# Two small rows of the setup asked for behind ScalarE's table load instead of ahead of it

## The chip, the cores and the metric

The kernel runs on one core of a Trainium2 chip. The metric is the device time of one execution in microseconds (us), the median of several. Beside it stand the span (first to last instruction) of one profiled execution, and its trace.

## The reference, cut to what matters

One decoded token attends over a K and a V cache of 8 heads x 65536 rows x 256 numbers, and a small gated block runs beside it:

```python
xn = _layernorm(x, axis=-1)                       # x: 448 numbers
return x + _A_ref(xn, k_cache, v_cache, wq, wo)   # attention: q = xn @ wq, softmax(q k) v, @ wo
         + _B_ref(xn, w_r, w_gate, w_up, w_down)  # gated block, scaled by sigmoid(xn @ w_r)
```

The caches alone are 537 MB. The two rows are `x` (A_x) and `w_r` (B_w_r), 448 bf16 numbers or 896 bytes each. All the queries need `x`; the setup also reads `w_r` early.

## The kernel before

Each engine has its own list of instructions. `W` makes an engine wait for a named event, `O` adds an operation that signals its name, "d" is a transfer. SyncE asks for the big blocks, first wq, then K in halves:

```python
    item("wq", [(wq_area, flat_src(A_wq, WQN), "wq")])
    for u in range(U):
        k_item(u)          # blocks 0 and 1 at once; blocks 2 and 3 when TensorE has read the half before
    v_item(0)
```

A K block is 8.39 MB, a half 4.19 MB. Blocks 2 and 3 take the buffers of 0 and 1, so SyncE can ask for a half of them only when TensorE has transposed the half that lies there. ScalarE asks for the rows and then takes the square root of the layer norm:

```python
    def act_setup():
        a = nc.scalar
        for k, (d, s) in enumerate([(x_row, A_x[0]), (wr_row, B_w_r.rearrange("(o n) -> o n", o=1))]):
            prog["act"].append(("d", here[0], ("w0", k), (d, s), "w0"))
        items["w0"] = ("w0", 32)
        W("act", "VPE")
        O("act", "SQRT", lambda it: a.activation(out=stat[0:1, 3:4], in_=stat[0:1, 2:3], func=ACTF.Sqrt), "evq")
        ...
```

VectorE waits for both rows, converts `x` (`xf`), normalises; TensorE turns the row into columns (XNT), multiplies by wq (QT), and VectorE writes the queries (`qT_sb`). Meanwhile GpSimd writes constants and, last, fills `kt_all` with zeros:

```python
        O("pool", "z_q", lambda it: v.memset(q_cur[:, :, :], 0.0))
        O("pool", "KZ", lambda it: v.memset(kt_all[:, :], 0.0))
```

## Time and profile before

| | before |
|---|---|
| time, median of 3 (range) | 1277.45 us (1277.29 to 1277.73) |
| span of the profiled run | 1275.9 us |
| bytes moved, mean rate | 549.2 MB, 430 GB/s |
| DMA engines busy, by fortieth of the span | 9 tenths or more in 39, 8 in the last |
| rows seen by VectorE; queries ready; first K transposes | 7.06; 17.39; 22.68 us |

The page cuts the span into 40 slices with a digit of busy tenths for each engine, and lists the chain of work that ended last. The timeline gives start, duration, engine, source line and tiles, and in brackets the idle time before with what ended it. "SPq" and "ACTq" are requests for transfers.

### The profile page before, as it was taken

The numbers are of one execution on the slowest core, as the hardware profiler recorded it, in microseconds if no ns is written. First come the engines' busy times: TensorE is split into PE (matmuls) and PEld (weight loads), VectorE is DVE, ScalarE is ACT, GpSimd is POOL, SyncE is SP. The second block draws the span as 40 slices with busy tenths as digits, with TensorE's granted clock in tenths as the row PEclk, the third lists the DMA queues.
The fourth block names the chain that finished last, engine by engine and source line by source line (L and its number), as shares of the span: only waits on it lengthen the run. The fifth ranks groups of instructions, "written<-read, shape, count | busy, mean of one in ns | idle before, by whom it ended". The sixth has DMA issues, their size and how long they took to land.

```text
span 1275.9 us, 23521 instructions
## 1 busy us (share of the span) xinstructions
PE 956.1 (75%) x9744; PEld 627.2 (49%) x9744; DVE 570.5 (45%) x1078; ACT 436.6 (34%) x655; POOL 8.0 (1%) x38
## 2 busy tenths in 40 slices
PE   3998977678767769777778677687777698777664
PEld 3676655445544446444455454454444565444331
DVE  4665544445434455444454344454444544444310
ACT  1554533244322433324233243343333334332300
POOL 2000000000000000000000000000000000000000
PEclk9998998889888899888899888898888988887877
DMA  9999999999999999999999999999999999999998
GB/s 405 428 438 427 443 431 434 434 434 434 434 431 436 434 436 431 434 436 429 434 436 434 434 434 431 436 434 431 436 431 436 434 431 436 431 434 434 424 431 355
DMA packets 12886, 549.20 MB, mean 430 GB/s; under 512 B 1351, under 2 KB 1994, under 8 KB 3402
## 3 DMA queue, kind: packets, MB, share of 16 engines
q1 hardware_dynamic: 12868, 549.03, 99.7%
q8 instruction: 8, 0.13, 0.0%
q14 instruction: 4, 0.03, 0.0%
q10 hardware_dynamic: 6, 0.00, 0.0%
HBM read 549.03 MB, written 0.00 MB: 430 GB/s over the span
## 4 chain that ended last, share of the span: by engine, by line
DMA 78%; PE 18%; ACT 2%; issue 1%; DVE 1%; SPq 0%; ACTq 0%; DVEq 0%
DMA ring<-in_A_v_cache_dram 69%; PE ps_o L418 12%; DMA ring<-in_A_k_cache_dram 5%; PE ps_t L418 3%; DMA kt_all<-in_A_wo_dram 3%; DMA ring<-in_A_wo_dram 2%; PE ps_q L418 2%; ACT kt_all L479 2%; PE ps_m L418 1%; SPq L918 0%; DVE kt_all L477 0%; ACT S_sb L560 0%; DVE kt_all L720 0%; PE ps_s L418 0%; DVE kt_all L823 0%
## 5 line engine op out<-in xcount | busy, mean ns | idle before, releaser
L418 PE MATMUL ps_t<-ident_f,ring 128*128 128x128 f32 x4096 | 588.0, 285 | 83.3 <-DMA ring<-in_A_k_cache_dram 62.1
L477 DVE COPY kt_all<-ps_t 128x1024 bf16<-128x1024 bf16 x768 | 487.0, 685 | 294.0 <-PE ps_q L418 289.9
L418 PEld LDWEIGHTS ps_t<-ident_f,ring 128*128 128x128 f32 x4096 | 451.6, 144 | 235.8 <-issue 134.7
L479 ACT ACTIVATE kt_all<-ps_t 128x1024 bf16<-128x1024 bf16 x256 | 262.2, 1024 | 500.4 <-PE ps_q L418 500.3
L418 PE MATMUL ps_o<-ring,p_sb 128*4 128x512 bf16 x2044 | 173.6, 500 | 205.9 <-DMA ring<-in_A_v_cache_dram 201.6
L418 PEld LDWEIGHTS ps_o<-ring,p_sb 128*4 128x4 bf16 x2044 | 54.0, 101 | 290.3 <-issue 262.7
L418 PE MATMUL ps_q<-kt_all,q_cur 128*2 128x512 bf16 x2056 | 164.5, 397 | 0.3 <-DVE kt_all L477 0.3
L501 ACT ACTIVATE s<-ps_q 98x512 bf16<-98x512 f32 x257 | 151.8, 591 | 1.3 <-PE ps_q L418 1.3
L583 DVE RECIPROCAL rs<-ps_m 128x4 f32<-128x4 f32 x29 | 5.3, 183 | 273.3 <-PE ps_m L418 273.3
L570 ACT ACTIVATE p_sb<-S_sb 128x128 bf16<-128x128 bf16 x64 | 18.9, 307 | 262.4 <-PE ps_o L418 262.2
L418 PEld LDWEIGHTS ps_s<-sel_bf,s 128*128 128x128 bf16 x1032 | 64.0, 97 | 5.0 <-ACT s L501 1.9
L418 PE MATMUL ps_s<-sel_bf,s 128*128 128x8 bf16 x1032 | 63.3, 167 | 1.3 <-ACT s L501 1.3
L636 DVE CAST ob_sb<-ps_o 100x512 bf16<-100x512 f32 x29 | 20.1, 692 | 88.6 <-PE ps_o L418 88.6
L418 PEld LDWEIGHTS ps_q<-kt_all,q_cur 128*2 128x2 bf16 x2056 | 26.4, 79 | 45.1 <-issue 45.1
L418 PEld LDWEIGHTS ps_m<-rowsum,ones_f 128*128 128x128 f32 x58 | 12.0, 260 | 21.5 <-issue 21.5
L479 ACT ACT_TABLE_LOAD x7 | 9.0, 1283 | 27.6 <-PE ps_q L418 27.6
L530 DVE TENSOR_REDUCE m1p<-S_sb (+1 forms) x33 | 13.9, 422 | 4.4
L418 PE MATMUL ps_m<-rowsum,ones_f 128*128 128x4 f32 x58 | 14.6, 322 | 0.0
L528 DVE CAST S_sb<-ps_s 128x256 f32 (+1 forms) x33 | 13.7, 416 | 1.9 <-PE ps_s L418 1.9
L560 ACT ACTIVATE S_sb<-S_sb,negmax 128x512 bf16<-128x512 bf16 x16 | 13.2, 852 | 3.2 <-DVE negmax L554 3.2
L418 PE MATMUL ps_m<-diag,ones_f 2*128 2x2 f32 x58 | 11.2, 260 | 3.8 <-DVE diag L545 0.8
L418 PEld LDWEIGHTS ps_m<-diag,ones_f 2*128 2x128 f32 x58 | 8.7, 187 | 10.6 <-DVE diag L545 10.6
(95 smaller groups left out, 133.2 us busy)
## 6 DMA issues: line engine op xcount, KB each, us to landing
ring<-in_A_k_cache_dram SPq DMA_DIRECT2D x10, 4096.0 KB, 28.5
ring<-in_A_v_cache_dram SPq DMA_DIRECT2D x1, 4096.0 KB, 26.7
ring<-in_A_wq_dram SPq DMA_DIRECT2D x1, 3584.0 KB, 11.6
ring<-in_A_wo_dram SPq DMA_DIRECT2D x1, 2688.0 KB, 28.1
ring<-in_A_v_cache_dram SPq DMA_DIRECT2D x1, 2048.0 KB, 30.9
ring<-in_B_w_gate_dram SPq DMA_DIRECT2D x1, 1568.0 KB, 16.3
ring<-in_B_w_up_dram SPq DMA_DIRECT2D x1, 1568.0 KB, 19.5
ring<-in_B_w_down_dram SPq DMA_DIRECT2D x1, 1568.0 KB
```

The costliest lines, as they stand in the source:

```text
L418: return pe.matmul(*a, **k)
L477: O(e, ("EV", s, m), lambda it: nc.vector.tensor_copy(out=kt[:, :], in_=tb[:, :]), f"ev{m}")
L479: O(e, ("EV", s, m), lambda it: nc.scalar.activation(out=kt[:, :], in_=tb[:, :], func=ACTF.Copy), f"ev{m}")
L501: O("act", ("EVQ", s), lambda it: nc.scalar.activation(out=s2[s % 2][0:QROWS, :], in_=ps_q[0:QROWS, :], func=ACTF.Copy), "evq")
L528: O("dve", ("SCOPY", u), lambda it: nc.vector.tensor_copy(out=S_sb[:, at(it, SBN), :], in_=ps_sn), "sc")
L530: O("dve", ("SMAX", u), lambda it: nc.vector.tensor_reduce(out=m1p[:, :, at(it, 1)], in_=S_sb[:, at(it, SBN), :].rearrange("p n i -> p i n ...
L560: O("act", ("EXP", h, i), lambda it, i=i: nc.scalar.activation(out=S_sb[:, :, i], in_=S_sb[:, :, i], func=ACTF.Exp, bias=negmax[:, i:i + 1 ...
L570: O("act", ("PC", t, c), lambda it: nc.scalar.activation(out=p_sb[:, c, :, :], in_=S_sb[:, n:n + CH, :], func=ACTF.Copy), "pc")
L583: O("dve", ("RS", t), lambda it: nc.vector.reciprocal(out=rs[:, :, :], in_=ps_m[0:P, C_TOT:C_TOT + NH * rep]))
L636: O("dve", ("OB", t), lambda it: nc.vector.tensor_copy(out=ob_sb[0:OROWS, :], in_=ps_o[0:OROWS, :]))
```

## The change

The intent is that the function table of the square root is loaded at the very start of ScalarE's list, by a square root of one number that nobody reads, and that the rows are asked for after it. The root signals the same event as the rows, so those who wait for the rows count to 33 instead of 32. Whole:

```diff
     def act_setup():
         a = nc.scalar
+
+        W("act", "ones")
+        O("act", "TABLE", lambda it: a.activation(out=stat[0:1, 8:9], in_=ones_f[0:1, 0:1], func=ACTF.Sqrt), "w0")
+        W("act", "TABLE")
         for k, (d, s) in enumerate([(x_row, A_x[0]), (wr_row, B_w_r.rearrange("(o n) -> o n", o=1))]):
             prog["act"].append(("d", here[0], ("w0", k), (d, s), "w0"))
-        items["w0"] = ("w0", 32)
+        items["w0"] = ("w0", 33)
         W("act", "VPE")
```

## The prediction

> **What bounds the kernel now.** I read the page's slices first, since they say whether one resource is busy in every stretch.
>
> ```profile
> DMA  9999999999999999999999999999999999999998
> GB/s 405 428 438 427 443 431 434 434 434 434 434 431 436 434 436 431 434 436 429 434 436 434 434 434 431 436 434 431 436 431 436 434 431 436 431 434 434 424 431 355
> DMA packets 12886, 549.20 MB, mean 430 GB/s; under 512 B 1351, under 2 KB 1994, under 8 KB 3402
> ```
>
> In all but the first and last slices the sixteen DMA engines move 424 to 443 GB/s. 549.2 MB at 434 GB/s take 1265 us of the 1275.9 us span; ramp and tail hold the other ten. So the bound is the stream of transfers that SyncE issues (wq, then K and V blocks), and a change counts only if this stream starts later, runs dry or ends later. Next, the chain of waits, in order of time, for where compute enters it early on.
>
> ```profile
> 1.19 21.45 DMA ring<-in_A_k_cache_dram
> 22.68 1.97 PE ps_t L418 x8
> ...
> 81.08 1.04 PE ps_t L418 x8
> 82.14 37.95 DMA ring<-in_A_k_cache_dram
> 120.13 1.97 PE ps_t L418 x8
> ```
>
> TensorE starts its first K block at 22.68 us because that block's first half has landed; at 82.14 the chain goes back to a transfer. From 22.68 to 82.14 it names PE steps, which looks like a compute-bound stage. The table by stretches (columns: width, then busy us and count of PE, PEld, DVE, ACT, POOL, then the TensorE clock, DMA share and GB/s) corrects that:
>
> ```profile
> 0.00:22.68 22.68, 3.54 (x122) 3.41 (x123) 8.88 (x24) 2.97 (x4) 8.04 (x38) 1.00 0.95 391
> 22.68:82.14 59.46, 56.87 (x560) 41.91 (x560) 39.46 (x68) 29.95 (x43) 0.00 (x0) 1.00 1.00 431
> ```
>
> The transfers run at 431 GB/s there too: TensorE is merely busy beside them while blocks wait in the buffers. The third view is the timeline of the setup, which is what the change touches.
>
> ```profile
> 0.73 0.53 ACTq L918 DMA_DIRECT2D ring<-in_A_x_dram  x1
> 0.74 0.39 SPq L918 DMA_DIRECT2D ring<-in_A_wq_dram  x1
> ...
> 1.29 0.21 ACTq L918 DMA_DIRECT2D ring<-in_B_w_r_dram  x1
> ...
> 1.53 1.28 ACT L398 ACT_TABLE_LOAD   x1 [1.53 <-PEq L1131]
> ...
> 5.21 3.51 POOL L349 MEMSET kt_all<- 128x4096 bf16 x1
> 7.06 1.90 DVE L361 CAST ring<-ring 1x448 f32<-1x448 bf16 x1 [2.87 <-DMA ring<-in_B_w_r_dram]
> ...
> 17.20 0.19 DVE L409 TENSOR_SCALAR qT_sb<-ps_m 128x32 bf16<-128x32 f32 x1 [3.39 <-PE ps_m L418]
> 22.68 1.57 PEld L418 LDWEIGHTS ps_t<-ident_f,ring 128*128 128x128 f32 x8 [5.68 <-DMA ring<-in_A_k_cache_dram]
> ```
>
> The reader is to see the chain from rows to queries: rows asked for at 0.73 and 1.29, both there at 7.06, normalised on VectorE, multiplied by wq, queries ready at 17.20 + 0.19 = 17.39. Nothing can use them before the first K half at 22.68. The slack is 22.68 - 17.39 = 5.3 us, and the chain is not the one that sets the end.
>
> [...] the w_r row's 896-byte packet starts at 5.60 us, between packets of wq at 1.06 us each and long before wq is through at about 12.3; the 4-byte packet that signals it follows at 6.70, one wq packet later. So a small row passes a long queue, but not at once. [...] The five SyncE issues of the start are over by 1.19 + 2.11 = 3.30 us[...]. [...] The 1.28 us is in the trace[...]:
>
> ```profile
> 123.14 1.28 ACT L479 ACT_TABLE_LOAD   x1 [6.21 <-PE ps_q L418]
> 124.43 1.02 ACT L479 ACTIVATE kt_all<-ps_t 128x1024 bf16<-128x1024 bf16 x1
> ```
>
> The next function starts 1.29 us after the load does; I use 1.29. [...] The 1.90 us cast fits: it ends at 8.96, just after GpSimd's 5.21 + 3.51 = 8.72, and the opposite cast of the same 448 elements took 0.38 us.
>
> **The change part by part.** *Added:* one square root of one element, 0.20 us by its twin in the group rows, and a wait for the ones that GpSimd writes at 0.87 + 0.20 = 1.07 us. *Not added:* a table load, since that of the real square root moves to the new one. In the kernel before, the load ran at 1.53 though its function waited until 11.12, so it isn't held by the wait; I expect it at about 0.74, ending at 2.02, by when the ones are written. The function then ends at about 2.03 + 0.20 = 2.23. *Moved:* the row issues wait for it. The first goes from 0.73 to about 2.3, the second from 1.29 to about 2.8[...].
>
> Now the landing. Before, x was ahead of wq on an idle engine: packet at 1.64, 0.9 us after its issue. w_r (ready at about 1.29 + 0.9 = 2.2) arrived during the first wq packet of its engine (1.76 to 3.46) and got in at 5.60, after the third. After the change x is ready at 2.3 + 0.9 = 3.2, still inside that first packet, so at best it takes the same turn, 5.60. Behind it in one queue stand its signal, the w_r row and that row's signal; at one per turn with a wq packet of 1.06 us between, they start at 6.7, 7.8 and 8.8. Before, the signal at 6.70 was seen by VectorE at 7.06, 0.36 us later; so the rows are there at about 9.2 us, an estimate, or 10.3 if x misses its turn. That is 2.1 to 3.2 us later, against 1.6 us by which the issue moved.
>
> Part comes back: at 9.2 GpSimd's fill is over, so the cast should take about 0.4 instead of 1.90 us and end at 9.6 instead of 8.96. The chain after it (mean, variance, root, transposes, wq product) is unchanged in lengths, so it is 0.6 us later, 1.7 in the bad turn: queries ready at 18.0 to 19.1, with 4.7 to 3.6 us left before 22.68. Sum on the path that sets the end: 0. [...] three or four tiny packets enter the busy stream at some 50 ns each on one of 16 engines[...].
>
> **The rivals.** *First: the rows queue behind everything that SyncE has asked for.* Then they land only with the last of the first 20.45 MB (wq 3.67, two K blocks 16.78), at 434 GB/s after about 49 us. Even then there are reserves after the queries. SyncE asks for the fourth K block's second half here:
>
> ```profile
> 70.72 0.33 SPq L918 DMA_DIRECT2D ring<-in_A_k_cache_dram  x1
> 71.17 0.35 SPq L918 DMA_DIRECT2D ring<-in_A_v_cache_dram  x1
> ```
>
> By 70.72 it had asked for 33.03 MB, of which 29.0 had moved by the packet records: 4.0 MB, or 9.3 us, were still queued. This is the least reserve of the first four blocks (15 us at the issue of 35.62). So the queries may be late by 5.3 + 9.3, about 14.6 us, before the stream runs dry at all. Full queueing puts the rows 42 us late: some 40 - 14.6 = 25 us more, 1303 us, 2% slower. Against it: w_r overtook two thirds of wq[...]. I give it 1%. [...]
>
> *Second: faster, because the table load is out of the way and the stream starts cleaner.* But the real square root never waited for its load (ended 2.81, used 11.12), and the stream starts with SyncE's issue at 0.74, which waits for nothing of ACT's. Worth at most 0.1 us.
>
> *Third: a colder or warmer TensorE at 22.68.* Its idle gap before the first K half shrinks from 5.6 to about 4 to 5 us. The first eight transposes took 1.97 us there and 1.09 when warm, so a microsecond or two of PE time could come or go; at 82 to 120 the TensorE waits for transfers anyway, so none of it reaches the end.
>
> **Range and chances.** Three runs before spread 0.44 us. With nothing on the path I predict 1277.4 us. I widen the range to 1276.4 to 1278.8 for a rebuilt program and a little of the late-row rival. Faster by over 2% 0.5%, within 2% 98.5%, slower by over 2% 1%.
>
> **What would show it.** ACT's load at about 0.74 and its row issues at 2.3 to 3.3 us; VectorE's first cast at 9.2 to 10.3 us and 0.4 long; queries at 18 to 19; the first K transposes still at 22.7, released by the transfer; the issue of 35.6 unmoved within a microsecond; DMA slices as before. I am wrong if the rows land after some 14 us, so that the first transposes wait for the queries, and wrong in the result if the DMA row then shows a dip before 140 us.

The record's sum on the path that sets the end came to 0 us, which gave the 1277.4. Cuts are marked; they take out two things of the forecast. One is a term for wq's request, which the record called too small to be timed, like the tiny packets (that request took 0.39 us; the rows' packets took 78 and 41 ns, those of their signals 9). The other is a half-way form of the first rival: rows at 15 to 25 us, a loss of 0 to 3 us, chance 5%. The sum stays 0. What the argument stands on is measured: w_r's packets at 5.60 and 6.70, beside wq packets of 1.06 us; 1.29 us from the start of a table load to the function behind it; a cast of 1.90 us that ended 0.24 us after GpSimd's fill, against 0.38 for the opposite one. That the fill held the cast was the author's estimate at this point. The 1% for the first rival stands on w_r's early packet. "Colder" and "warm" are the record's words for eight transposes that took 1.97 us at 22.68 and 1.06 to 1.09 between 30 and 80 us of the same trace; the granted clock was 1.00 in both stretches, and the cause is not shown.

## More of the kernel before

After QT TensorE sets the registers of its big loop and enters it; the loop's first matmuls are transposes of the first K half:

```python
            for k, rk in enumerate(regs):
                ...
                if rk != "tmp":
                    eng.reg_mov(pool[k], rk[0])
            ...
                with eng.Fori(0, n * period) as it:
```

## The result

The changed kernel took 1277.75 us (median of 6 runs, 1277.58 to 1278.00) against 1277.55 (6 runs, 1277.29 to 1277.89). The ratio is the mean of one kernel's fast runs over that of the other's of the same rounds, so it isn't quite the ratio of these medians: 1.0001, 95% interval 0.9989 to 1.0014. The time is the same. The span of the profiled run is 1275.6 against 1275.9.

The timeline of the changed kernel's setup:

```profile
0.73 1.28 ACT L396 ACT_TABLE_LOAD   x1 [0.73 <-PEq L1135]
...
2.02 0.20 ACT L396 ACTIVATE stat<-ones_f 1x1 f32<-1x1 f32 x1
2.25 0.52 ACTq L922 DMA_DIRECT2D ring<-in_A_x_dram  x1
...
2.81 0.21 ACTq L922 DMA_DIRECT2D ring<-in_B_w_r_dram  x1
...
9.51 0.38 DVE L361 CAST ring<-ring 1x448 f32<-1x448 bf16 x1 [5.32 <-DMA ring<-in_B_w_r_dram]
...
18.14 0.19 DVE L413 TENSOR_SCALAR qT_sb<-ps_m 128x32 bf16<-128x32 f32 x1 [3.39 <-PE ps_m L422]
23.59 1.57 PEld L422 LDWEIGHTS ps_t<-ident_f,ring 128*128 128x128 f32 x8 [5.65 <-DMA ring<-in_A_k_cache_dram]
```

The load runs first, the rows are asked for 1.52 us later than before and seen 2.45 us later (9.51 against 7.06), the cast is short (0.38 against 1.90), and the queries are ready at 18.33, only 0.94 us later. All this is as predicted. The last line is not: the first K transposes start at 23.59, not at 22.7. The bracket says that the transfer ended the wait. The chain of waits of the same run, in order of time, says otherwise:

```profile
1.19 21.75 DMA ring<-in_A_k_cache_dram
22.94 0.68 issue
23.62 1.94 PE ps_t L422 x8
```

The K half was there at 22.94; then comes 0.68 us of "issue", time in which TensorE waited for nothing that the profile shows. Still nothing reaches the end. SyncE's request for the second half of the fourth K block, the one with the least reserve in the prediction, came at 71.79 us, 1.07 later than the 70.72 of before:

```profile
71.79 0.33 SPq L922 DMA_DIRECT2D ring<-in_A_k_cache_dram  x1
```

(Not even that can be put to the rows: table_only and fill_early below, whose rows are on time, have 71.77.) The slices of the transfers show no dip:

```profile
DMA  9999999999999999999999999999999999999998
GB/s 404 430 435 434 440 432 430 436 430 440 434 430 436 430 440 434 432 432 434 432 438 434 430 436 430 442 432 432 432 434 434 440 430 432 434 430 442 417 435 355
```

So two questions were left for the experiments. How large is the reserve really, as the time alone shows only that it is larger than what the change takes? And what is the "issue" time before the first transposes, where the prediction saw 5.3 us of slack?

### The profile page after: what moved, and what is told of

It is laid out like the page before. It is cut to its first block, busy times and chain, and to the rows that moved or that the text cites. A ratio compares the mean times of both kernels' runs of the same rounds, so it can differ in the third digit from the quotient of the medians.

```text
span 1275.6 us, 23522 instructions
## 1 busy us (share of the span) xinstructions
PE 957.5 (75%) x9744; PEld 625.2 (49%) x9744; DVE 568.4 (45%) x1078; ACT 436.8 (34%) x656; POOL 8.1 (1%) x38
## 4 chain that ended last, share of the span: by engine, by line
DMA 78%; PE 18%; ACT 2%; issue 1%; DVE 1%; SPq 0%; ACTq 0%; DVEq 0%
DMA ring<-in_A_v_cache_dram 68%; PE ps_o L422 13%; DMA ring<-in_A_k_cache_dram 5%; DMA kt_all<-in_A_wo_dram 3%; PE ps_t L422 3%; DMA ring<-in_A_wo_dram 2%; PE ps_q L422 2%; ACT kt_all L483 2%; PE ps_m L422 1%; SPq L922 0%; DVE kt_all L481 0%; ACT S_sb L564 0%; DVE kt_all L724 0%; PE ps_s L422 0%; DVE kt_all L827 0%
## 5 line engine op out<-in xcount | busy, mean ns | idle before, releaser
L422 PE MATMUL ps_o<-ring,p_sb 128*4 128x512 bf16 x2044 | 180.0, 514 | 207.8 <-DMA ring<-in_A_v_cache_dram 203.4
L483 ACT ACT_TABLE_LOAD x7 | 9.0, 1283 | 23.4 <-PE ps_q L422 23.4
```

What stands on the lines that cost most here:

```text
L422: return pe.matmul(*a, **k)
L483: O(e, ("EV", s, m), lambda it: nc.scalar.activation(out=kt[:, :], in_=tb[:, :], func=ACTF.Copy), f"ev{m}")
```

## The experiments

Beside the kernel before, twelve kernels ran (the changed one is the first), all with correct results. "Queries" is the end of the instruction that writes them, "start" that of TensorE's first K transposes. "K3b request" is SyncE's request named above. The last column is the median time less that of the kernel before. Kernels are compared only within the same rounds.

| run | edit | rows seen | queries | start | K3b request | time |
|---|---|---|---|---|---|---|
| before | | 7.06 | 17.39 | 22.68 | 70.72 | |
| changed | | 9.51 | 18.33 | 23.59 | 71.79 | +0.20 |
| table_only | root added, rows ahead | 7.18 | 17.39 | 23.49 | 71.77 | -0.16 |
| wait_only | rows held, no root | 9.51 | 18.33 | 23.48 | 72.25 | +0.06 |
| fill_early | GpSimd's fill earlier | 7.08 | 15.91 | 22.97 | 71.77 | -0.07 |
| moves_early | changed, register moves earlier | 10.23 | 19.05 | 23.74 | 73.49 | -0.07 |
| late_sel | rows held to 5.3 | 11.70 | 20.52 | 26.07 | 74.18 | +0.20 |
| late_fill | rows held to 8.8 | 17.41 | 26.22 | 32.01 | 82.97 | +3.66 |
| late_wq | rows held to 12 | 19.89 | 28.70 | 33.37 | 82.19 | +5.95 |
| late_k0 | rows held to 21.5 | 29.61 | 38.42 | 43.02 | 93.91 | +16.62 |
| late_k1 | rows held to 51 | 52.51 | 61.32 | 63.74 | 114.11 | +36.75 |
| rows_first | rows on SyncE, ahead of wq | 4.12 | 16.14 | 23.40 | 72.91 | +0.54 |

(before_again and late_k0_moves, one look each, are told below. The runs of one "late" kernel differ by 2.0 to 3.9 us; the kernel before, over all its runs, by less than 1.)

### The two parts alone: table_only and wait_only

```diff
 table_only (from the kernel before)
         items["w0"] = ("w0", 32)
+        W("act", "ones")
+        O("act", "TABLE", lambda it: a.activation(out=stat[0:1, 8:9], in_=ones_f[0:1, 0:1], func=ACTF.Sqrt))
 wait_only (from the kernel before)
+        W("act", "sel", 0, 1)
         for k, (d, s) in enumerate([(x_row, A_x[0]), (wr_row, ...
```

> The added square root alone, with the row issues still ahead of it. If the lateness of the rows in the changed kernel comes from the moved issues alone: rows seen by VectorE at 7.06 us as in the kernel before, cast 1.9 us, queries at 17.4, first K transposes at 22.7, span unchanged (1275.9, within 0.4), time 1277.6. Rival, that the extra function or its wait is what delays the chain: queries 0.2 us or more later than 17.4.

> The row issues held until about 2.2 us by a wait on GpSimd's second selector copy, with no added square root and no earlier table load. If only the moment of the issue counts: issue at about 2.3, rows seen at 9.4 to 9.6 (four turns of one DMA engine, as in the changed kernel), cast 0.38 us, queries at 18.3, first K transposes at about 23.6, released by TensorE's own sequencer and not by the transfer; time 1277.7. Rival, that the earlier table load is what matters: rows at 7.1, first transposes at 22.7.

Ratios: 0.9999 (0.9982 to 1.0016) and 1.0001 (0.9985 to 1.0018). The wait alone gives the changed kernel's chain to the hundredth: rows at 9.51, queries at 18.33. The root alone leaves the queries at 17.39. So the lateness of the rows comes from the moment of asking alone. But table_only missed in one number: with its queries on time, the start was 23.49, not 22.7. Its timeline:

```profile
7.18 1.78 DVE L361 CAST ring<-ring 1x448 f32<-1x448 bf16 x1 [2.99 <-DMA ring<-in_B_w_r_dram]
...
17.20 0.19 DVE L411 TENSOR_SCALAR qT_sb<-ps_m 128x32 bf16<-128x32 f32 x1 [3.39 <-PE ps_m L420]
23.49 1.57 PEld L420 LDWEIGHTS ps_t<-ident_f,ring 128*128 128x128 f32 x8 [6.48 <-DMA ring<-in_A_k_cache_dram]
```

and its chain has the same idle piece, 0.69 us of "issue", after a landing at 22.83. So late rows are not needed for a late start. The second trace of the unchanged kernel was taken for this (the "instruction fetch" of its expectation is a packet that moves_early below tells of):

> The kernel before once more, for a second trace. If the 0.9 us by which the changed kernel starts its K work later is mostly the turn of the instruction fetch: the start lies anywhere from 22.6 to 23.7 us here, with the queries at 17.4 within 0.2. If it is the lateness of the rows: 22.7 again within 0.1.

It started at 22.91 with its queries at 17.43: neither the 22.7 within 0.1 of one theory nor clear of it, within the range of the other. Here the K half landed at 22.87, and TensorE was released by it, as in the first trace (22.64 and 22.68).

### The cast: fill_early

```diff
         O("pool", "z_zero", lambda it: v.memset(zero_bf[:, :], 0.0))
+        O("pool", "KZ", lambda it: v.memset(kt_all[:, :], 0.0))
         ...
         O("pool", "z_q", lambda it: v.memset(q_cur[:, :, :], 0.0))
-        O("pool", "KZ", lambda it: v.memset(kt_all[:, :], 0.0))
```

> The kernel before with GpSimd's 3.5 us fill moved ahead of the identity and selectors, so that it is over before the rows land; rows issued as before. If the 1.90 us cast was blocked by that fill: cast 0.38 to 0.5 us at 7.06, so queries about 1.4 us earlier, 15.9 to 16.1, unless wq (landed at 12.3) or the selectors hold them; first K transposes stay at 22.7 because the transfer is then the later one; time 1277.6. Rival, that the cast is slow for another reason (rows just landed, its first use): cast again 1.9 us, queries at 17.4.

```profile
1.16 3.51 POOL L328 MEMSET kt_all<- 128x4096 bf16 x1
...
7.08 0.38 DVE L361 CAST ring<-ring 1x448 f32<-1x448 bf16 x1 [2.89 <-DMA ring<-in_B_w_r_dram]
...
22.97 1.57 PEld L418 LDWEIGHTS ps_t<-ident_f,ring 128*128 128x128 f32 x8 [7.45 <-DMA ring<-in_A_k_cache_dram]
```

With the fill out of the way the same cast at the same moment takes 0.38 us. The 1.90 us of before was GpSimd's fill, as predicted, and the changed kernel's short cast is the fill being over by 9.51. The queries came 1.48 us earlier, and here the transfer did release TensorE (landed 22.93, start 22.97). The time is the same, ratio 1.0001 (0.9984 to 1.0017): early queries are worth nothing.

### What stands between the queries and the loop: moves_early and late_k0_moves

The trace shows that TensorE's sequencer, behind the last matmul of QT in its list, sets registers, 88 ns apart (24 recorded moves, 16.60 to 18.72 in the kernel before), and then has one branch of 3.12 us (18.77 to 21.89). The first theory was that the moves are what counts. The edit, shortened:

```diff
+            yield                      # in loop(), behind the register moves
 ...
+        if e == "pe":                  # in emit(), ahead of everything
+            ahead = loop([en for en in entries if en[1][0] == "K"], LOOPS["pe"]["K"])
+            next(ahead)                # does the moves now; the loop itself is run off later
```

> The changed kernel, with TensorE's register moves for its first loop (27 of them, some 88 ns apart, 2.4 us) done at the start instead of between the query products and the loop. Theory B (the first transposes of the changed kernel wait for TensorE's own moves and loop branch): first transposes 0.6 to 0.7 us earlier, at the landing of the first K half, 22.6 to 23.0; time unchanged at 1277.7, since the transfer stream has 9 us in reserve. Theory A (they wait for the transfer, as the record says): first transposes stay at 23.6.

Twenty-two of the moves now ran from 0.8 us on, and the theory fell: start at 23.74, landing 23.13, and again 0.64 us of "issue" behind it. The branch started 1.2 us earlier than in the changed kernel (18.50 against 19.71) although that run's rows were later, but it took 4.97 us instead of 3.55. What does fit is in the records of the transfers. Shortly before the start of the loop there is one packet of 16384 bytes in the queue that the page calls "q8 instruction". From the trace's records (us):

```
run            branch        packet        branch's end less packet's end
before         18.77 + 3.12  19.50 + 0.97  1.42
table_only     18.78 + 4.38  20.75 + 0.97  1.44
changed        19.71 + 3.55  20.86 + 0.97  1.43
fill_early     17.29 + 3.68  18.59 + 0.96  1.42
moves_early    18.50 + 4.97  21.05 + 0.97  1.44
late_fill      27.61 + 4.07  29.26 + 0.99  1.43
late_k0        39.81 + 2.88  40.23 + 1.03  1.43
late_k0_moves  37.80 + 5.01  40.34 + 1.04  1.43
late_k1        62.71 + 0.70  60.63 + 1.38  1.40
```

In all fourteen traces (nine are shown) the branch ends 1.40 to 1.44 us after that packet, wherever it begins. So TensorE seems to enter its loop when this packet, a 16 KB block of instructions by the queue's name, has come (a "fetch" below). That the branch waits for it is the reading of these times; what makes the block necessary there is not shown. The branch took 2.7 to 5.0 us in every trace but one. The last row of the table is the telling one. There SyncE had nothing queued (its last transfer had landed at 50.74); the packet moved before the branch began, and the branch took 0.70 us. On busy engines the packet came 0.3 to 2.6 us after the branch had begun. That it waits for its turn, as the rows seem to, would fit but is not shown, since no record tells when the block is asked for. The theory was then put to the test with an expectation of its own, on a run where TensorE is late anyway:

> The kernel with the rows behind the first K half, with TensorE's 27 register moves done at the start. Theory F (what separates the queries from the first transposes is one 16 KB fetch of instructions that waits for its turn on a busy DMA engine; the branch ends 1.4 us after that packet): moves gone, still 4.4 to 5.6 us from queries to first transposes. Theory B (the moves): 2.4 us less than the 4.6 of the twin run, 2.2 us.

The chain of waits of late_k0, then that of late_k0_moves:

```profile
38.12 4.93 issue
```

```profile
38.06 5.05 issue
```

From the queries to the start it was 4.72 us with the moves gone and 4.60 with them: the 22 moves, 1.9 us of them, made no difference beside the fetch.

### How late the rows may be: late_sel, late_fill, late_wq, late_k0, late_k1

Each holds the row requests of the kernel before until an event; the edit is one line above the requests:

```diff
+        W("act", "sel2", 3, 1, 1)       # late_sel: GpSimd's last selector
+        W("act", "KZ")                  # late_fill: GpSimd's last fill
+        W_item("act", "wq")             # late_wq: wq has landed
+        W_item("act", ("k", 0, 0))      # late_k0: first K half has landed
+        W_item("act", ("k", 1, 1))      # late_k1: second K block has landed
```

The parts of the first two expectations are estimates from two traces. In the changed kernel x was asked for at 2.25 and its first packet came at 5.91, the four packets of the rows started 1.06 to 1.10 us apart (the 1.2 below is generous), and the rows were seen 0.34 us after the last one started. In the kernel before, with nothing else queued, the first packet came 0.91 us after the request for x and 1.02 after that for wq.

> The kernel before with the row issues held until GpSimd's last fill, 8.8 us. Rows expected at about 16.7 (0.9 to be ready, about 3 behind what its DMA engine has taken, three turns of 1.2, 0.36 to be seen), queries 8.8 later at 25.5. Theory B (start of K work = queries + 5.2, against a landing at 22.7): first transposes at 30.7, 8.0 late; reserve of the transfer stream 9.3, so time unchanged, 1277.6 within 0.5. Theory A (queries may be 5.3 late for nothing): first transposes at about 25.6; time unchanged too. The two differ in the start, not the time.

> Row issues held until wq has landed, 12.3 us. Rows at about 20.3, queries 29.1, 11.7 late. Theory B: first transposes at 34.3, 11.6 late; reserve 9.3, and about 1 us from issue to first packet when the queue is empty, so the transfers run dry for 2 to 3.5 us before 90 us: 1280 to 1281. Theory A: reserve 14.6 in lateness of the queries, so nothing: 1277.6. Rival C (a dry spell is caught up later): a dip in the transfers, but 1277.6.

> Row issues held until the first K half has landed, 22.7 us. Rows at about 30.8, queries 39.6, 22.2 late. Theory B: first transposes at 44.8, 22.1 late; transfers dry for 22.1 - 9.3 + about 1 = 13 to 14 us: 1290.5 to 1291.5. Theory A: 22.2 - 14.6 + 1 = 8 to 9 us: 1286. Rival C: 1277.6.

> Row issues held until the whole second K block has landed, about 52.3 us, when the DMA engines are idle. Rows then need no turns: seen about 1.8 us after the issue, 54; queries 63; first transposes 68, 45.4 late. Theory B: dry for 45.4 - 9.3 + 1 = 36 to 38 us: 1314 to 1316, about 2.9% slower. Theory A: 32 us: 1309. This is the row-behind-everything rival of the record, made on purpose (it said 1303).

Ratios: late_fill 1.0027 (1.0012 to 1.0042), late_wq 1.0053 (1.0039 to 1.0066), late_k0 1.0133 (1.0117 to 1.0148), late_k1 1.0291 (1.0275 to 1.0306). Each lost more than theory A, the slack of the record, allows; theory B was right for late_k1, but 2.3 to 3.4 us short in the other three. Its fixed 5.2 us from the queries to the start measured 5.8, 4.7, 4.6 and 2.4 us. Rival C is out: the table by stretches (columns as in the prediction) shows the transfers running slow between 50 and 100 us, in the order before, late_fill, late_k0,

```profile
50.00:100.00 50.00, 48.06 (x493) 35.82 (x491) 35.26 (x60) 27.35 (x39) 0.00 (x0) 1.00 1.02 440
```

```profile
50.00:100.00 50.00, 47.20 (x470) 34.97 (x470) 32.88 (x56) 25.19 (x35) 0.00 (x0) 0.97 0.94 393
```

```profile
50.00:100.00 50.00, 45.88 (x457) 34.24 (x456) 32.73 (x57) 25.03 (x36) 0.00 (x0) 0.97 0.73 296
```

and what is lost stays lost. By the packet records late_k0 had moved its first 100 MB 15.3 us after the kernel before, and its first 540 MB 15.9 us after it; its span is 15.7 longer. The size of the reserve comes from the profiled runs. How late the K3b request is, less how much the span grows, is what the lateness did not cost: late_fill (82.97 - 70.72) - (1281.11 - 1275.88) = 12.25 - 5.23 = 7.0; late_wq 11.47 - 4.35 = 7.1; late_k0 23.19 - 15.69 = 7.5; late_k1 43.39 - 36.34 = 7.1. (In the second trace of the kernel before the request came at 71.06, so a few tenths are noise.) Among these four runs every further microsecond of lateness costs about one.

The packet records split what was lost. The packets' times, added up and divided by the 16 engines, fill 1272.64 us of the span before, 1274.28 in late_fill and 1274.22 in late_k0; the changed kernel and late_sel have 1272.54 and 1272.51. So of the 5.23 us that late_fill lost, 3.59 are idle engines and 1.64 are packets that took longer. By idle time alone the reserve is 12.25 - 3.59 = 8.7 us, and 8.8, 9.1 and 9.1 in the other three. No run lies between a lateness of 3.46 us (late_sel) and 11.47 (late_wq), so whether loss begins at 7 us or nearer 9 is not shown. With the 7 us a dose below the reserve was predicted:

> The row issues held until GpSimd's last selector, 5.3 us: a delay between the changed kernel (2.3) and the first that lost time (8.8). Rows at about 13, queries at 21.8 to 22.1, first transposes 4.7 to 5.8 later at 26.5 to 27.9, issue of the fourth K block's second half at 75.5 to 78.5 against 70.7. Theory D (time = lateness of that issue less 7.1 us, as the four late runs give it, and never below zero): 1277.5, at most 1278.3, and the transfers not dry. Theory A' (any lateness of the queries is paid from the first microsecond once TensorE waits for them): 1277.5 + 4 to 5 = 1282.

```profile
11.70 0.38 DVE L361 CAST ring<-ring 1x448 f32<-1x448 bf16 x1 [7.50 <-DMA ring<-in_B_w_r_dram]
...
26.07 1.57 PEld L419 LDWEIGHTS ps_t<-ident_f,ring 128*128 128x128 f32 x8 [5.94 <-issue]
```

Rows, queries and start came 0.4 to 1.3 us earlier than expected. Three of its four runs took 1277.52 to 1277.63, the fourth 1280.44; ratio 1.0009 (0.9992 to 1.0026). The K3b request of the profiled run is 3.46 late and costs nothing, so theory D holds there, and A' falls. The one slow run has no trace. Whether late fetches used up part of the reserve there is not shown; in late_fill the "issue" piece before the start (at 25.92) was 6.12 us long, only 0.3 us more than the same stretch in the profiled late_sel (20.22 to 26.07), so what the slow run lost its 2.9 us to stays open. late_k1, where SyncE has nothing queued and the rows were seen 1.75 us after the request for x (50.76 to 52.51), has

```profile
61.02 2.75 issue
```

in the same place. Its start came 4.3 us before the expected 68 (2.6 from this shorter way into the loop, 1.7 from queries that were early), while its time was right: errors of the expectation, in the start and in what came after it, largely cancelled.

### Rows ahead of everything: rows_first

The edit, shortened:

```diff
+    item("w0", [(x_row, A_x[0], "w0"), (wr_row, B_w_r.rearrange("(o n) -> o n", o=1), "w0")])
     item("wq", [(wq_area, flat_src(A_wq, WQN), "wq")])
 ...
-        for k, (d, s) in enumerate(...)      # the two requests of ScalarE
```

> Both rows asked for by SyncE ahead of wq, none by ScalarE. Rows there at about 3 us, so no row can be late; but the stream of wq and K starts behind two issues, at about 2.7 instead of 1.76. If the start of the stream counts one for one and early rows are worth nothing: queries at 16.6 (held by wq's landing, 13.2, plus 3.4), first transposes at the landing of the first K half, about 23.7, span and time 0.9 longer, 1278.4. Rival (early rows are worth something that the late rows took): 1277.4 or less.

```profile
1.40 0.36 SPq L916 DMA_DIRECT2D ring<-in_A_wq_dram  x1
...
23.40 1.57 PEld L416 LDWEIGHTS ps_t<-ident_f,ring 128*128 128x128 f32 x8 [7.65 <-DMA ring<-in_A_k_cache_dram]
```

The stream starts 0.66 us later, not 0.9 (the two requests took less than assumed), and the time is 0.54 us longer; the ratio 1.0004 (0.9987 to 1.0021) calls it the same, but the four runs (1277.88 to 1278.09) all lie above the seven of the kernel before (1277.26 to 1277.58). The direction is as expected and the size is not. Rows that are there at 4 us buy nothing. No run pointed to a version that beats both kernels.

## Why the prediction was right, and where it was not

- **The bound.** Right. The stream of transfers sets the end: holding the rows moved nothing as long as the stream stayed full and moved the end one for one once it ran dry.
- **Table load, requests, landing.** Right: load at 0.73 and over at 2.01, function at 2.02, requests at 2.25 and 2.81 (said 0.74, 2.02, 2.03, 2.3, 2.8). The packets of x, its signal, w_r and its signal started at 5.91, 7.01, 8.07 and 9.17 (said 5.6, 6.7, 7.8, 8.8), one turn of about 1.1 us apart; rows at 9.51 (said 9.2 to 10.3). wait_only confirms that the moment of asking is the whole cause.
- **The cast.** Right, 0.38 us (said 0.4), with fill_early to show why.
- **"Nothing can use them before the first K half at 22.68. The slack is 22.68 - 17.39 = 5.3 us."** This step was wrong. It took the landing of the K half for the only thing between the queries and the loop, because the view named the transfer. TensorE's own way into the loop (to the end of its second branch) takes until 4.2 to 5.9 us after the queries on busy DMA engines. In the two traces of the kernel before that branch ended at 22.03 and 22.33, some 0.6 and 0.5 us ahead of the landing at 22.64 and 22.87; in table_only it ended after the landing (23.30 against 22.83). There is practically no slack.
- **"the first K transposes still at 22.7, released by the transfer".** Wrong for the same reason: 23.59, and by the packet records after the fetch (packet over at 21.83, branch at 23.26), not at the landing at 22.94. How much of the 0.9 us is the rows' lateness is not settled: table_only has a start as late with rows on time.
- **The reserve, 4.0 MB "or 9.3 us".** Right in kind and nearly in size: by idle time it is 8.7 to 9.1 us. Queued bytes over rate leaves out the start of a new transfer (1.02 us from wq's request at 0.74 to its first packet in the kernel before). What the working did not have is that in runs that went dry the packets took 1.6 to 2.0 us longer in sum, so that only 7.0 to 7.5 us of the lateness went unpaid. And lateness grew on its way: in late_fill from 9.3 us at the start to 12.25 at the K3b request, with a piece of 1.50 us of "issue" at 49.65 in between. That this is a further fetch is the author's estimate: in the kernel before, such a piece (39.53 to 40.19) ended 1.4 us after a 16384-byte packet (37.75 + 1.06).
- **"late by 5.3 + 9.3, about 14.6 us, before the stream runs dry at all".** Wrong, as the first term is not there: queries 8.8 us late (late_fill) already cost 3.7 us, those 3.1 late (late_sel) nothing in three runs of four. The change's 0.94 is well inside.
- **The rivals.** The first was rightly ruled out, as the rows were seen at 9.51, before wq landed at 11.9; but made on purpose by late_k1 it costs 36.75 us, not 25. Its half-way form, rows at 15 to 25 us for 0 to 3 us, was too cheap as well: rows at 17.41 (late_fill) cost 3.66 us and at 19.89 (late_wq) 5.95. The third, another pace of TensorE at its start, did not come: the first eight transposes took 1.94 us against 1.97.

The result came out because the second reserve alone, at least the 3.46 us that late_sel used for nothing and some 7 us by the runs that lost, is larger than the lateness of about a microsecond that the change passes on. The first reserve, in which the record saw the whole change absorbed, was not there. The record had named the second one too, but only as what lies behind the first; that the time did not show the missing first one was luck as far as that step goes.

## What to carry to other kernels

To say that a delay is hidden, follow it to the resource that bounds the kernel and measure the reserve there, by delaying the thing on purpose in steps until the time moves; the idle time at the first waiter is not a reserve, for the engine may have work of its own left that the view doesn't count. A wait that the view puts down to a transfer can have been ended by the engine's own sequencer: compare the landing with the start (22.94 and 23.59 in the changed kernel), and look for "issue" between them in the chain. Beside a full stream the small transfers here, rows and a block of instructions, came late (3.6 to 4.6 us from a row's request to its first packet, 0.3 to 2.6 us from the branch's start to the block's), so don't count on their time; but asking for the rows ahead of the stream cost 0.54 us here and gained nothing.

## What else the traces show

- Beside a full stream of transfers the branch that ends 1.40 to 1.44 us after the 16384-byte packet took 2.7 to 5.0 us in thirteen traces, and 0.70 where SyncE had nothing queued (late_k1). These packets are on queue 8; queue 14 has only packets of 8192 bytes and smaller.
- The first K half landed at 22.6 to 23.1 us in the seven traces where the block moved before it was through (packet of 0.97 us at 18.6 to 21.1) with wq asked for at 0.74, and at 21.5 to 21.8 in the six where it moved later. Why is not shown; no run was made for it alone.
- A row of 896 bytes and the 4 bytes that signal it moved as packets 1.10 us apart in the changed kernel, where a wq packet took 1.06 us, and the first of them came 3.6 to 4.6 us after the request (x at 2.25 to 5.91 in the changed kernel and at 8.75 to 13.31 in late_fill, w_r at 1.29 to 5.60 in the kernel before).
- Two gaps next to a table load of 1283 ns were only 11 and 17 ns long. The changed kernel's function starts 11 ns after its load ends (0.730 + 1.283 and 2.024), and in the kernel before a load starts 17 ns after the function ahead of it ends (1206.623 and 1206.640).
- In the four runs that ran dry the packets took longer: their summed time per engine is 1.6 to 2.0 us above the 1272.64 us of the kernel before; why is not shown.
